# Normalization, the 1e-9 and three weight rebases moved to POOL in a windowed-attention stage

## The chip, the cores and the metric

The kernel runs on one NeuronCore of a Trainium2 chip. The metric is the device time of one execution in microseconds; less is better. A core has TensorE (PE in the profile), VectorE (DVE), ScalarE (ACT), GpSimd (POOL) and SyncE (SP), which here only issues transfers. Each engine runs its own instructions in order; between engines there are semaphores.

## The reference

Attention with a window of the last 96 positions and 8 global ones, then two feed-forward blocks:

```python
scores = scale * np.matmul(q, k.transpose(0, 1, 3, 2)) + bias      # masked to local | global
scores = scores - np.max(scores, axis=-1, keepdims=True)
a = np.exp(scores)
a = a / (np.sum(a, axis=-1, keepdims=True) + 1e-09)
x = np.matmul(a, v)                    # (2, 8, 768, 64) -> 1536 tokens x 512
h = x @ w_in                           # 512 -> 2048
g = np.where(h > 0.0, h, np.exp(np.minimum(h, 0.0)) - 1.0)
x = g @ w_out                          # 2048 -> 512
h = np.maximum(np.maximum(x @ w1, x @ w2), x @ w3)
out = h @ w_out2                       # 512 -> 768 -> 512
```

The weights arrive as 64-bit floats. The chip gets them as pairs of 32-bit words, rebuilds a 32-bit float from each pair and splits it into a high and a low part, whose products with the split activations make up the full-precision product.

## The kernel before, in words

**Attention steps.** The work is 48 steps; a step is one block of 128 queries of one head pair. The first 18 (k = 0 to 17) run in a loop of their own in `windowed` (from line 897), the first attention stage; the rest is woven into the feed-forward blocks by `run`, where TensorE has the long products. The schedule is manual: each engine gets its instructions in the order in which the code is written.

In the first stage a step is spread over four passes of the loop. In pass k TensorE makes the scores of step k in PSUM (`scores_pe`, L217), the product with the values of step k-3 (`values_pe`, L316) and the transposes of step k-2 (`turn_pe`, L287 or L293). DVE adds the biases and takes the row minimum (`scores_dve`, L243, one custom instruction and a short accumulator read for each of the two heads), forms the reciprocal of the sums of step k-1 (`recip`, L255), multiplies the exponentials of step k-1 by it (`norm`, L277, two instructions) and subtracts the rounded part of the output of step k-3 (`values_low`, L332). ACT rounds that output (`values_high`, L326), copies the transposes out of PSUM (`turn_act`, L304), exponentiates (`scores_act`, L264, with the row sums as accumulators) and adds 1e-9 to the two sums (`sums`, L226). POOL scales the queries of a later head pair every other step (`scale_queries`, L187).

**Weight conversion.** From pass 7 on, the generator `convert` hands out one piece per pass, for weight chunks 0, 1 and 2 (each 128 x 2 x 512 pairs of words). `c_rebase` (L404) multiplies the high words by a power of two, on ACT; `c_low` (L408) prepares the low words, on DVE; two `c_word` (L415, DVE, one long instruction each) join them and need the rebased high words; `c_high` (L423, ACT) rounds the high part; `c_rest` (L428, DVE) subtracts. The pieces fall so: pass 7 rebase and low of chunk 0; 8 and 9 the words; 10 high of 0 with rebase and low of 1; 11 word; 12 rest of 0; 13 word; 14 high of 1 with rebase and low of 2; 15 rest of 1; 16 and 17 words of 2. "High words" and "low words" are two interleaved halves of one buffer, so a rebase reads and writes every other 32-bit word.

**Later.** The products (L505) begin in pass 16. In the first feed-forward block POOL subtracts `gl` (L517), and conversion goes on there with rebases on ACT.

SP issues the loads in written order; query and key loads (`raw`), value loads (`v`) and weight chunks (`wr`) share its queue.

Of the kernel before, what the change touches and what calls it, by code (L numbers as in the profile page):

```python
# [16 lines left out]
AF = mybir.ActivationFunctionType  # L17
ALU = mybir.AluOpType
# [29 lines left out]
def numbers(nc, pool, n_ap):  # L48

    ni = pool.tile([P, 4], I32, name="ni")  # L50
    nc.sync.dma_start(ni, n_ap.bitcast(I32).partition_broadcast(P))
    w = pool.tile([P, 4], F32, name="nw")
    nc.vector.tensor_copy(w, ni)
    w2 = w.rearrange("p (a b) -> p a b", b=2)
    hi = pool.tile([P, 2], F32, name="nhi")
    nc.vector.scalar_tensor_tensor(
        hi, w2[:, :, 0], 0.0, w2[:, :, 1], op0=ALU.is_lt, op1=ALU.add
    )
    nf = pool.tile([P, 2], F32, name="nf")
    nc.vector.scalar_tensor_tensor(  # L60
        nf, hi, 4294967296.0, w2[:, :, 0], op0=ALU.mult, op1=ALU.add
    )
    return nf[:, 0:1], nf[:, 1:2]


def covered(nc, pool, ng, nl, flag):

    f = pool.tile([P, 4], F32, name="nok")
    nc.vector.tensor_scalar(f[:, 0:1], ng, 0.0, None, op0=ALU.is_ge)
    nc.vector.tensor_scalar(f[:, 1:2], ng, float(G), None, op0=ALU.is_le)  # L70
    nc.vector.tensor_scalar(f[:, 2:3], nl, 1.0, None, op0=ALU.is_ge)
    nc.vector.tensor_scalar(f[:, 3:4], nl, float(PREV + 1), None, op0=ALU.is_le)
    ok = pool.tile([P, 1], F32, name="ok")
    nc.vector.tensor_reduce(ok, f, axis=AX.X, op=ALU.min)
    nc.vector.tensor_copy(flag, ok)
# [33 lines left out]
class Windowed:  # L109
# [110 lines left out]
                )  # L220
            self.s_t[s] = [x[:, o:o + n] for x in sp]

    def sums(self, k):
        if k in self.p_t:
            m = self.p_t[k][1]
            self.nc.scalar.activation(m[:, 4:6], m[:, 2:4], AF.Copy, bias=1e-9)  # L226

    def scores_dve(self, k, early=False, other=-1):

# [36 lines left out]
                accum_out=m[:, 2 + u:3 + u],  # L266
            )

    def norm(self, k):
        if k not in self.p_t:  # L270
            return
        nc = self.nc
        n = self.geom(k)[-1]
        p, m = self.p_t[k]
        for u in range(2):
            o = slice(u * WIN, u * WIN + n)
            nc.vector.tensor_scalar(p[:, o], p[:, o], m[:, 6 + u:7 + u], None, op0=ALU.mult)  # L277

    def turn_pe(self, k, tag="TX"):
        if k not in self.p_t:  # L280
# [77 lines left out]
class Feed:  # L358
# [39 lines left out]
            return [(self.whole[c], slice(0, 2))]  # L398
        return [(self.wraw[j], j % 2) for j in (2 * c, 2 * c + 1) if j in self.wraw and c < NFC]

    def c_rebase(self, c):
        for r, _ in self.parts(c):
            a = r[..., 1].bitcast(F32)
            self.nc.scalar.activation(a, a, AF.Copy, scale=2.0 ** -112)  # L404

    def c_low(self, c):
        for r, _ in self.parts(c):
# [441 lines left out]
def windowed(tc, ctx, io, flag):  # L849
    nc = tc.nc  # L850
    f = Feed(tc, ctx, io)
    at = Windowed(tc, ctx, io, f.ps, f.xy, f.wt, f.act)
    with tc.manual_schedule():
        scratch = [f.cv.tile([P, 512], F32, tag="wr", name="sc") for _ in range(2)]
        at.load_pair(0, True)
        f.warm(WARM)
        at.positions(scratch)
        ng, nl = numbers(nc, at.const, io["nn"])
        for p in range(1, 3):
            at.load_pair(p, True)  # L860
        at.scale_queries(0)
        at.bases(ng, nl, 0, P + WIN)
        first = BLOCKS[0] // GRP * 8
        x = f.split_tiles()

        def convert():
            f.c_rebase(0)
            f.c_low(0)
            yield
            f.c_word(0, 0)  # L870
            yield
            f.c_word(0, 1)
            yield
            f.c_high(0)
            f.c_rebase(1)
            f.c_low(1)
            yield
            f.c_word(1, 0)
            yield
            f.c_rest(0)  # L880
            yield
            f.c_word(1, 1)
            yield
            f.c_high(1)
            f.c_rebase(2)
            f.c_low(2)
            yield
            f.c_rest(1)
            yield
            f.c_word(2, 0)  # L890
            yield
            f.c_word(2, 1)
            yield

        words = convert()
        h = f.ps.tile([P, 512], F32, tag="h", name="h")
        for k in range(first + 2):
            e = k % 2
            at.load_values(k, True)
            if e == 0:  # L900
                at.load_pair(k // 2 + 3, k < first)
                at.scale_queries(k // 2 + 1)
            if k <= first:
                at.scores_pe(k, (("S0", "S1"), ("y0", "y1"))[e], 1 + (k == first))
            if k >= first:
                f.product(h, f.w[0][:, 0], x, GRP, 0, (k - first) * 6, 6)
            at.values_pe(k - 3)
            at.turn_pe(k - 2, ("TX", "y2", "y3")[k % 3])
            if k < FILL[0]:
                f.fill(at.ident, FILL[1])  # L910
            at.scores_dve(k, True)
            at.values_high(k - 3, x)
            at.turn_act(k - 2, nc.scalar.copy)
            at.scores_act(k)
            at.sums(k)
            at.recip(k - 1)
            at.norm(k - 1)
            at.values_low(k - 3, x)
            if k >= CONV:
                next(words, None)  # L920
            if k in WLOAD:
                f.w_load()
        at.values_pe(first - 1)
        at.turn_pe(first, "TX")
        at.values_high(first - 1, x)
        at.turn_act(first, nc.scalar.copy)
        at.values_low(first - 1, x)
        at.recip(first + 1)
        at.norm(first + 1)
        next(words, None)  # L930
        f.run(at, first + 2, x, h, lambda: covered(nc, at.const, ng, nl, flag))


def build(tc, io):
    nc = tc.nc
    with tc.tile_pool(name="flag", bufs=1) as fp:
        flag = fp.tile([P, 1], I32, name="fast")
        with ExitStack() as ctx:
            windowed(tc, ctx, io, flag)
        fast = nc.values_load(flag[0:1, 0:1], min_val=0, max_val=1)  # L940
        with tc.If(fast < 1):  # L941
            with tc.tile_pool(name="xd", bufs=1, space=bass.MemoryType.DRAM) as dp:
                xd = dp.tile([NT // GRP, P, NCC, GRP], F32, name="xd")
                with ExitStack() as ctx:
                    dense_attention(tc, ctx, io, xd)
                with ExitStack() as ctx:
                    f = Feed(tc, ctx, io)
                    with tc.manual_schedule():
                        f.w_load()
                        f.w_load()  # L950
                        f.w_load()
                        for c in range(2):
                            f.c_rebase(c)
                            f.c_low(c)
                            f.c_word(c, 0)
                            f.c_word(c, 1)
                            f.c_high(c)
                            f.c_rest(c)
                        f.c_rebase(2)
                        f.c_low(2)  # L960
                        f.c_word(2, 0)
                        f.c_word(2, 1)
                        f.run(Stored(nc, f.xy, xd), 0)
# [73 lines left out]
```

## Time and profile before

| | |
|---|---|
| three runs | 569.23, 574.21, 575.95 us (median 574.21) |
| profiled execution | span 569.0 us; its own time is not listed beside the span |
| PE busy | 549.6 us (97%) |
| DVE busy | 315.4 us (55%) |
| ACT busy | 277.1 us (49%) |
| POOL busy | 78.3 us (14%) |
| first attention stage | about the first 50 us of the span |

The span runs from the first to the last instruction on the core. Busy shares are averages over the whole of it; the stage that is changed is less than a tenth. In rows of a timeline the first number is the start in microseconds from the span's start, the second the duration, and what stands in brackets at the end is the idle time of the engine before it and who ended it.

### The profile page before, as it was taken

To read this page: it belongs to the slowest core of one execution; us is meant where nothing else is said; L and a number is where in the kernel's file an instruction comes from. 1 tells how busy PE (TensorE), PEld (TensorE's weight loads), DVE (VectorE), ACT (ScalarE), POOL (GpSimd) and SP (SyncE) were. 2 spreads that over 40 slices of the span, in tenths; PEclk is the share of its full clock that TensorE was granted. 3 is DMA by queue.
4 is the path that set the end of the run, shared out by engine and by line. 5 is a ranking of instruction groups with operands and counts; after the bars stand their busy time and mean duration, and the time that the engine had idled before them with its cause. 6 is when DMAs were issued, how large, how long until landed. Compare 5 with 4: busy or idle time off the path is not lost. (4 is left out here: it accounts for less than half of the span.)

```text
span 569.0 us, 7586 instructions
## 1 busy us (share of the span) xinstructions
PE 549.6 (97%) x2772; PEld 435.0 (76%) x2772; DVE 315.4 (55%) x684; ACT 277.1 (49%) x622; POOL 78.3 (14%) x87
## 2 busy tenths in 40 slices
PE   8799999999999999999999999999999999999995
PEld 6467777776777777778888888888887888888884
DVE  6987999999745333333466656567754112312112
ACT  5988777777656555554555554524323101311011
POOL 4100222222210000000011222023320000000000
PEclk9969999999999999999999999999999999999999
DMA  8919444532211111010013223122302000010002
GB/s 293 381 45 345 166 168 137 181 122 78 67 36 42 42 41 43 20 55 1 0 38 111 88 98 111 37 75 77 117 29 75 1 1 0 8 67 1 0 1 79
DMA packets 16669, 46.61 MB, mean 82 GB/s; under 512 B 1776, under 2 KB 1776, under 8 KB 16624
## 3 DMA queue, kind: packets, MB, share of 16 engines
q1 hardware_dynamic: 15760, 44.47, 22.8%
q10 hardware_dynamic: 864, 1.57, 0.8%
q8 instruction: 24, 0.39, 0.3%
q14 instruction: 21, 0.17, 0.1%
HBM read 42.90 MB, written 3.15 MB: 81 GB/s over the span
## 5 line engine op out<-in xcount | busy, mean ns | idle before, releaser
L505 PE MATMUL h<-xh,w 128*128 128x512 f32 (+1 forms) x536 | 144.5, 391 | 0.8 <-ACT xh L485 0.8
L505 PEld LDWEIGHTS h<-xh,w 128*128 128x128 f32 x536 | 98.1, 188 | 24.5 <-issue 1.8
L536 PE MATMUL y<-gh,w 128*128 128x512 f32 x384 | 98.6, 399 | 0.0
L512 ACT CAST gh<-e 128x512 fp32r<-128x512 f32 x66 | 41.0, 622 | 101.8 <-DVE e L725 87.4
L536 PEld LDWEIGHTS y<-gh,w 128*128 128x128 f32 x384 | 69.7, 188 | 18.1 <-ACT e L526 1.7
L725 DVE TENSOR_TENSOR e<-S,e 128x512 f32<-128x512 f32 x36 | 24.9, 692 | 103.5 <-PE S L505 100.8
L505 PE MATMUL h<-xl,w 128*128 128x512 f32 (+1 forms) x268 | 81.8, 386 | 0.0
L505 PE MATMUL S<-xh,w 128*128 128x512 f32 x288 | 77.0, 389 | 0.0
L530 DVE SCALAR_TENSOR_TENSOR e<-e,h 128x512 f32<-128x512 f32 x48 | 33.0, 687 | 67.7 <-ACT e L526 67.7
L505 PEld LDWEIGHTS S<-xh,w 128*128 128x128 f32 x288 | 54.1, 188 | 11.2
L525 ACT ACTIVATE e<-h 128x512 f32<-128x512 f32 x48 | 28.7, 597 | 65.2 <-PE h L505 63.0
L462 POOL TENSOR_TENSOR w<-wr,w 128x512 fp32r<-128x512 f32 x24 | 35.4, 1474 | 166.1 <-ACT w L461 166.1
L505 PEld LDWEIGHTS h<-xl,w 128*128 128x128 f32 x268 | 50.0, 188 | 10.3
L517 DVE TENSOR_TENSOR gl<-e,gh 128x512 fp32r<-128x512 f32 x50 | 39.8, 796 | 31.8 <-ACT gh L512 31.6
L264 ACT ACTIVATE p<-p,m 128x232 f32<-128x232 f32 (+1 forms) x96 | 44.8, 469 | 24.4 <-DVE m L243 24.4
L544 PE MATMUL y<-gl,w 128*128 128x512 f32 x192 | 51.5, 390 | 0.0
L415 DVE SCALAR_TENSOR_TENSOR wr<-wr 128x1024 uint32<-128x1024 uint32 (+1 forms) x36 | 49.9, 1395 | 0.8 <-ACT wr L404 0.2
L505 PE MATMUL S<-xl,w 128*128 128x512 f32 x144 | 44.3, 389 | 0.0
L451 DVE SCALAR_TENSOR_TENSOR wr<-wr 128x512 uint32<-128x512 uint32 x48 | 43.0, 896 | 2.2
L544 PEld LDWEIGHTS y<-gl,w 128*128 128x128 f32 x192 | 36.0, 188 | 7.9 <-issue 0.3
L569 PE MATMUL y<-w,gh 128*128 128x512 f32 x144 | 37.3, 390 | 0.4 <-POOLq L941 0.4
L517 POOL TENSOR_TENSOR gl<-e,gh 128x512 fp32r<-128x512 f32 x16 | 21.0, 1310 | 104.3 <-ACT gh L512 104.3
(85 smaller groups left out, 604.4 us busy)
## 6 DMA issues: line engine op xcount, KB each, us to landing
wr<-wa SPq DMA_DIRECT2D x14, 1024.0 KB, 6.4
wr<-wb SPq DMA_DIRECT2D x24, 512.0 KB, 3.3
v<-v SPq DMA_DIRECT2D x24, 256.0 KB, 2.8
raw<-qk SPq DMA_DIRECT2D x16, 312.0 KB, 3.1
raw<-qk SPq DMA_DIRECT2D x8, 260.0 KB, 3.3
wr<-wa SPq DMA_DIRECT2D x4, 512.0 KB, 3.8
out<-ot ACTq DMA_DIRECT2D x6, 256.0 KB, 2.6
out<-ot SPq DMA_DIRECT2D x6, 256.0 KB, 2.5
```

The costliest lines, as they stand in the source:

```text
L264: self.nc.scalar.activation(p[:, o], p[:, o], AF.Exp, bias=m[:, u:u + 1], scale=-1.0, accum_out=m[:, 2 + u:3 + u],)
L415: self.nc.vector.scalar_tensor_tensor(r[..., 0], r[..., 1], v, r[..., 0], op0=op, op1=ALU.bitwise_or)
L451: self.nc.vector.scalar_tensor_tensor(t, a, c, t, op0=op, op1=ALU.bitwise_or)
L462: nc.gpsimd.tensor_tensor(w[:, j % 2, 1], v, w[:, j % 2, 0].bitcast(F32), op=ALU.subtract)
L505: nc.tensor.matmul(out[:, o:n], w[:, part % 2, c * P:c * P + P], (xl if part == 2 else xh)[:, c, o:n], start=c == 0 and part == 0, stop=c ...
L512: self.nc.scalar.copy(gh[:, 0:n], e[:, 0:n])
L517: (engine or self.nc.vector).tensor_tensor(gl[:, 0:n], e[:, 0:n], gh[:, 0:n].bitcast(F32), op=ALU.subtract)
L525: self.nc.scalar.activation(e, h, AF.Relu, scale=-1.0)
L530: self.nc.vector.scalar_tensor_tensor(e, e, -1.0, h, op0=ALU.add, op1=ALU.max)
L536: self.nc.tensor.matmul(y[e][:, 0:n], w[:, a, e * P:e * P + P], g[0][:, 0:n], start=fc == 0 and a == 0, stop=False,)
L544: self.nc.tensor.matmul(y[e][:, 0:n], w[:, 0, e * P:e * P + P], g[1][:, 0:n], start=False, stop=fc == NFC - 1,)
L569: nc.tensor.matmul(o[r], gh[:, r * P:r * P + P], w[:, a], start=j == 0 and a == 0, stop=False,)
```

## The change

In the loop of the first stage `sums`, `norm` and `c_rebase` get a flag that puts their instructions on POOL, as a tensor-scalar instruction with two operations; the operations are the same (add 1e-9, multiply by the reciprocal, multiply by 2 to the -112). `norm` of step k-1 now stands ahead of `sums` of step k in the written order. Steps from 18 on, and the normalization of step 17, which stands after the loop, are as before.

```diff
-    def sums(self, k):
+    def sums(self, k, early=False):
         if k in self.p_t:
             m = self.p_t[k][1]
-            self.nc.scalar.activation(m[:, 4:6], m[:, 2:4], AF.Copy, bias=1e-9)
+            if early:
+                self.nc.gpsimd.tensor_scalar(
+                    m[:, 4:6], m[:, 2:4], 1e-9, 1.0, op0=ALU.add, op1=ALU.mult
+                )
+            else:
+                self.nc.scalar.activation(m[:, 4:6], m[:, 2:4], AF.Copy, bias=1e-9)
...
-    def norm(self, k):
+    def norm(self, k, early=False):
...
-            nc.vector.tensor_scalar(p[:, o], p[:, o], m[:, 6 + u:7 + u], None, op0=ALU.mult)
+            if early:
+                nc.gpsimd.tensor_scalar(
+                    p[:, o], p[:, o], m[:, 6 + u:7 + u], 1.0, op0=ALU.mult, op1=ALU.mult
+                )
...
-    def c_rebase(self, c):
+    def c_rebase(self, c, early=False):
         for r, _ in self.parts(c):
             a = r[..., 1].bitcast(F32)
-            self.nc.scalar.activation(a, a, AF.Copy, scale=2.0 ** -112)
+            if early:
+                self.nc.gpsimd.tensor_scalar(
+                    a, a, 2.0 ** -112, 1.0, op0=ALU.mult, op1=ALU.mult
+                )
+            else:
+                self.nc.scalar.activation(a, a, AF.Copy, scale=2.0 ** -112)
...
-            f.c_rebase(0)
+            f.c_rebase(0, True)
...
-            f.c_rebase(1)
+            f.c_rebase(1, True)
...
-            f.c_rebase(2)
+            f.c_rebase(2, True)
...
             at.scores_act(k)
-            at.sums(k)
             at.recip(k - 1)
-            at.norm(k - 1)
+            at.norm(k - 1, True)
+            at.sums(k, True)
             at.values_low(k - 3, x)
```

POOL before: in the whole first stage its program holds the setup and then nothing but the query scalings, which run as far ahead as their loads allow.

```order
L103 MEMSET qsc 64x1 x8
masks.py:197 MEMSET ident 128x128
masks.py:199 AFFINE_SELECT ident<-ident 128x128
L187 TENSOR_SCALAR raw<-raw,qsc 128x256 x10
L517 TENSOR_TENSOR gl<-e,gh 128x512 x2
```

POOL now, from pass 6 to pass 10 (L283 is `norm`, L227 `sums`, L417 `c_rebase` in the changed file):

```order
L187 TENSOR_SCALAR raw<-raw,qsc 128x256
L283 TENSOR_SCALAR p<-p,m 128x232 x2
L227 TENSOR_SCALAR m<-m 128x2
L283 TENSOR_SCALAR p<-p,m 128x128 x2
L227 TENSOR_SCALAR m<-m 128x2
L417 TENSOR_SCALAR wr<-wr 128x1024
L187 TENSOR_SCALAR raw<-raw,qsc 128x256
L283 TENSOR_SCALAR p<-p,m 128x232 x2
L227 TENSOR_SCALAR m<-m 128x2
```

The scalings are now one per two steps among two normalizations and an addition per step, and a rebase stands between the addition of step 7 and the scaling and normalization of pass 8.

DVE before, in the second half of pass 7 and at the start of pass 8:

```order
L243 ISA p,m<-y_318,rel 128x232 [waits PE_49]
L243 ISA m 128x1
L255 RECIPROCAL m<-m 128x2 [waits Activation_49]
L277 TENSOR_SCALAR p<-p,m 128x128 [waits DVE_49]
L277 TENSOR_SCALAR p<-p,m 128x128
L332 TENSOR_TENSOR xl<-TX,xh 128x128 [waits Activation_49]
L408 TENSOR_SCALAR wr<-wr 128x1024 [waits DMAHW0_49]
L243 ISA p,m<-S_348,rel 128x232 [waits PE_49]
```

DVE now, from the conversion of pass 7 through pass 8 (L425 is `c_low`, L248 the scores, L260 `recip`, L344 `values_low`, L432 `c_word`):

```order
L425 TENSOR_SCALAR wr<-wr 128x1024 [waits DMAHW0_49]
L248 ISA p,m<-S_348,rel 128x232 [waits PE_49]
L248 ISA m 128x1
L248 ISA p,m<-S_349,rel 128x232 [waits PE_49]
L260 RECIPROCAL m<-m 128x2 [waits Pool_49]
L344 TENSOR_TENSOR xl<-y_323,xh 128x128 [waits Activation_49]
L432 SCALAR_TENSOR_TENSOR wr<-wr 128x1024 [waits DVE_49,Pool_49]
L248 ISA p,m<-y_373,rel 128x232 [waits PE_49]
```

The two normalizations are gone from DVE, its reciprocal waits for POOL where it waited for ACT, and the word conversion of pass 8 waits for POOL.

## Rows read from the trace of the kernel before

**Rows 1.** Stretches: us, busy of PE, PEld, DVE, ACT, POOL; PEclk, DMA share, GB/s.

```profile
10.00:20.00 10.00, 9.37 (x80) 5.44 (x78) 8.88 (x48) 9.76 (x41) 1.23 (x3) 1.00 1.04 405
20.00:30.00 10.00, 6.06 (x53) 3.73 (x54) 9.42 (x32) 9.38 (x30) 2.02 (x3) 1.00 0.82 315
30.00:40.00 10.00, 10.00 (x54) 6.08 (x53) 9.04 (x35) 7.58 (x26) 0.00 (x0) 0.52 0.16 60
```

**Rows 2.** Timeline of DVE, step 12, to the start of step 13.

```profile
30.10 0.39 DVE L243 CUSTOM_DVE_ANT_0 p<-S,rel 128x232 f32<-128x232 f32 x1
...
30.73 0.16 DVE L255 RECIPROCAL m<-m 128x2 f32<-128x2 f32 x1
30.93 0.59 DVE L277 TENSOR_SCALAR p<-p,m 128x232 f32<-128x232 f32 x2
31.44 0.28 DVE L332 TENSOR_TENSOR xl<-y,xh 128x128 fp32r<-128x128 f32 x1
31.64 1.22 DVE L428 TENSOR_TENSOR w<-wr,w 128x1024 fp32r<-128x1024 f32 x1
32.77 0.39 DVE L243 CUSTOM_DVE_ANT_0 p<-y,rel 128x232 f32<-128x232 f32 x1
```

**Rows 3.** Timeline of DVE: starts of steps 5, 7, 10 and 11, and ends.

```profile
13.80 0.39 DVE L243 CUSTOM_DVE_ANT_0 p<-y,rel 128x232 f32<-128x232 f32 x1
...
17.11 0.39 DVE L243 CUSTOM_DVE_ANT_0 p<-y,rel 128x232 f32<-128x232 f32 x1
...
24.75 0.39 DVE L243 CUSTOM_DVE_ANT_0 p<-S,rel 128x232 f32<-128x232 f32 x1
...
26.29 0.69 DVE L408 TENSOR_SCALAR wr<-wr 128x1024 uint32<-128x1024 uint32 x1
26.89 0.39 DVE L243 CUSTOM_DVE_ANT_0 p<-y,rel 128x232 f32<-128x232 f32 x1
...
47.59 0.28 DVE L332 TENSOR_TENSOR xl<-y,xh 128x128 fp32r<-128x128 f32 x1
```

**Rows 4.** Timeline of ACT and of DVE: an addition and a wait.

```profile
23.72 0.20 ACT L226 ACTIVATE m<-m 128x2 f32<-128x2 f32 x1
...
40.90 0.29 DVE L332 TENSOR_TENSOR xl<-y,xh 128x128 fp32r<-128x128 f32 x1 [1.40 <-ACT xh L326]
```

**Rows 5.** POOL: one line's durations (min/median/max ns), and an iota.

```profile
L187 POOL TENSOR_SCALAR raw<-raw,qsc x10: 477/522/934, 4.0 to 26.4; 128x256 f32<-128x256 f32 x10
...
1.67 0.14 POOL L79 IOTA rel<- 128x8 f32 x1
```

**Rows 6.** Timeline of DVE and POOL: conversions alone and beside POOL.

```profile
23.62 1.22 DVE L415 SCALAR_TENSOR_TENSOR wr<-wr 128x1024 uint32<-128x1024 uint32 x1
...
58.36 1.95 DVE L415 SCALAR_TENSOR_TENSOR wr<-wr 128x1024 uint32<-128x1024 uint32 x1
...
26.39 0.93 POOL L187 TENSOR_SCALAR raw<-raw,qsc 128x256 f32<-128x256 f32 x1 [1.02 <-DMA raw<-qk]
...
57.94 1.29 POOL L517 TENSOR_TENSOR gl<-e,gh 128x512 fp32r<-128x512 f32 x1 [5.27 <-ACT gh L512]
59.20 1.45 POOL L187 TENSOR_SCALAR raw<-raw,qsc 128x256 f32<-128x256 f32 x1
```

**Rows 7.** Timeline of PE: value products of five passes.

```profile
20.96 0.44 PE L316 MATMUL y<-p,v 128*64 128x128 f32 x4 [1.00 <-ACT p L304]
...
22.80 0.66 PE L316 MATMUL TX<-p,v 116*64 116x128 f32 x8 [0.22 <-ACT p L304]
...
24.71 0.66 PE L316 MATMUL y<-p,v 116*64 116x128 f32 x8
...
29.26 0.66 PE L316 MATMUL y<-p,v 116*64 116x128 f32 x8 [1.97 <-ACT p L304]
...
31.55 1.12 PE L316 MATMUL TX<-p,v 116*64 116x128 f32 x8
...
34.71 1.12 PE L316 MATMUL y<-p,v 116*64 116x128 f32 x8
```

More of the change, by code (lines that the diff above doesn't have):

```diff
@@ L276, in norm @@
             o = slice(u * WIN, u * WIN + n)
-            nc.vector.tensor_scalar(p[:, o], p[:, o], m[:, 6 + u:7 + u], None, op0=ALU.mult)
+            if early:
[3 more added lines that the diff above has]
+            else:
+                nc.vector.tensor_scalar(
+                    p[:, o], p[:, o], m[:, 6 + u:7 + u], None, op0=ALU.mult
+                )
     def turn_pe(self, k, tag="TX"):
@@ L399, in parts @@
         return [(self.wraw[j], j % 2) for j in (2 * c, 2 * c + 1) if j in self.wraw and c < NFC]
-    def c_rebase(self, c):
+    def c_rebase(self, c, early=False):
         for r, _ in self.parts(c):
             a = r[..., 1].bitcast(F32)
-            self.nc.scalar.activation(a, a, AF.Copy, scale=2.0 ** -112)
+            if early:
+                self.nc.gpsimd.tensor_scalar(
+                    a, a, 2.0 ** -112, 1.0, op0=ALU.mult, op1=ALU.mult
+                )
+            else:
+                self.nc.scalar.activation(a, a, AF.Copy, scale=2.0 ** -112)
     def c_low(self, c):
```

## The prediction, made before the changed kernel was run

> **What bounds the kernel now.** I read the table of 10 us windows first. After the first stage, which ends near 50 us, TensorE paces the kernel; the change touches only the 18 steps before. There [rows 1] ACT is busy 9.76 of 10 us between 10 and 20, DVE and ACT 9.4 each between 20 and 30, and between 30 and 40 TensorE is full, but at a granted clock of 0.52 (its lower level, 1.2 GHz); POOL is nearly free, and the DMA share falls from 1.04 to 0.16. So the bound changes hands: ACT up to step 7, then DVE, then TensorE at its low clock.
>
> Steps are read off DVE's first score instruction. Early ones go in pairs of 3.31 us, 13.80 to 17.11. From step 7 (17.11) each holds one weight-conversion instruction. A step with a long one (a word or a rest) [rows 2]: scores 0.63 us, reciprocal 0.20, two normalizations 0.51, `values_low` 0.20, conversion 1.13, together 2.67. One with the short `c_low` takes 2.14, from 24.75 to 26.89 [rows 3]. From step 7 to the last conversion's end at 47.59 are 30.48 us; three short and eight long steps would be 27.78. The 2.70 over are stalls, among them 1.40 in which DVE waited for ACT [rows 4], which had a weight cast and a rebase in front.
>
> **The sum is made on the profiled span.** That is 569.0 us; the profiled execution's own time is not listed apart from it. The span lies 0.2 under the fastest of the three times and 5.2 under their median, 574.21, to which I carry the difference. Within 1% (5.7 us) is about what a measurement of this kernel cannot tell from no change; the three times themselves spread by 6.7.
>
> **Part 1: what leaves DVE and ACT.** Seventeen steps lose 0.51 us of normalizing on DVE (the eighteenth stays there), eighteen a 0.20 us addition on ACT, and three a rebase on ACT [rows 2, 4]. In steps 3 to 6, ACT-bound, 0.2 a step comes off: **-0.8 us**. The bounds are 0 and -1.0: the longer way recip, normalize, transpose, next scores, can eat it.
>
> **Part 2: what POOL pays, and the port.** A 128x256 scaling in the same form (one tensor, a per-partition scalar, two operations) takes 0.477 us at its shortest [rows 5], so a 128x232 normalization about 0.44, two of them 0.8. The addition on two columns I put at the 0.14 of an iota on eight [rows 5]. The price depends on what POOL and DVE do to each other. Look at the three instructions at 58 us [rows 6]: DVE's word conversion, 1.22 us when alone, took 1.95 from 58.36, and ended 1.08 after POOL's 1.29 us subtraction ended at 59.23. POOL's next scaling was issued at 59.20 and ended 0.34 after the conversion did. At 26.39 a POOL scaling took 0.93 and ended 0.34 after DVE's `c_low` of 26.29 [rows 3, 6]. So the two shut each other out, instruction by instruction: the later one waits, loses about 0.14 less than the whole wait, and a waiting DVE instruction comes before POOL's next. DVE's scores, which read PSUM, ran beside POOL's subtraction unhurt.
>
> Now a long step by that rule, time 0 at the end of reciprocal(k-1). POOL normalizes head 0 from 0.1 to 0.55. DVE does `values_low` and reaches its conversion at 0.2, held until 0.55, and done 1.08 later at 1.63. Head 1 ends 0.34 after that, at 1.97, the addition at 2.1. DVE's next scores end at 2.18, reciprocal(k) at about 2.35. The step shrinks from 2.67 to 2.35, not to the 2.16 that removing 0.51 promises. With `c_low` it is 1.9 against 2.14. Eight times 0.32 and three times 0.24: **-3.3 us**. If POOL instead finished both heads before DVE got in, a long step would be 2.7 and this term near 0; if nothing collided, 8 x 0.51 + 3 x 0.51 = -5.6.
>
> The rows price a pair of normalizations at 0.8 us on POOL against 0.51 on DVE [rows 2, 5]. The Trainium skill, "GPSIMD Engine Reference", section 4.1, leaves elementwise work to VectorE, but calls POOL with one input roughly line-rate; at one element a cycle of its 1.2 GHz (section 1) a head would be an estimated 0.2 us, a long step about 2.1, and the sum 2 us lower. The trace's 0.477 us for 256 columns speaks against line rate. That POOL and VectorE share their SBUF interfaces (section 8) the 1.95 us shows.
>
> **Part 3: stalls that go.** The 2.70 us of stalls from step 7 on came from ACT's casts plus rebases and from the low clock. With the rebases gone from ACT they go: **-2.7 us** (the clock is a term of its own below). If only the 1.40 goes, -1.4.
>
> **Part 4: rebases on POOL.** A rebase is 1024 elements with a stride of 8 bytes. Four times 0.477 is 1.9 us; four times the 0.34 a released scaling needed, plus a start of 0.14, is 1.5; I take 1.65. The order says what waits. In step 7 the rebase follows the addition of step 7, which needs its exponentials, about 2.0 after reciprocal(6); so it runs from 2.0 to 3.65. Behind it on POOL stand the query scaling (0.48, every other step), normalization 7, addition 8. On DVE the word conversion of step 8 waits for the rebase itself, and reciprocal(8) for addition 8. After 3.65: scaling to 4.1, conversion to about 5.1, head 0, head 1, addition to 5.9, reciprocal done at 6.1. Step 8 therefore takes about 4.05 us instead of 2.35. Step 11 has no scaling: 3.75. Step 15's rest does not need the rebase's result, but meets it at the port: 3.75. Extra: 1.7 + 1.4 + 1.4, and 0.3 because the addition ends late in steps 7 and 10: **+4.8 us** (bounds +2.5, if POOL's rebase takes 1.0 us less than I think, to +8, if DVE waits out 2.6 us, twice the 1.29 of the 512-column subtraction).
>
> "GPSIMD Engine Reference", section 7, of the Trainium skill gives POOL reads of at most 8 bytes a step about 1.9 cycles per element and larger ones about 2.9; at 1.2 GHz an estimate of 1.6 or 2.5 us for this rebase, whose step is exactly 8 bytes. No run here shows a strided one; by 2.5 the sum would be 2.5 us higher.
>
> **Part 5: the clock.** A TensorE step takes 1.91 us at full clock (22.80 to 24.71) and 3.16 at half (31.55 to 34.71); it fell between 29.26, where an idle gap of 1.97 us ended, and 31.55 [rows 7], and was low to about 40 (0.52 in that stretch, [rows 1]). In step 8 of the changed kernel TensorE has done its values and sits about 2 us until normalization 7. The nearest row is that gap, so I assume one fall as before: step 9 costs 3.16 for 2.35, step 10 3.16 for 1.9, step 11 is slower anyway. **+2.1 us** (0 to +7).
>
> **Nothing else.** POOL's query scalings move behind the additions; the last was done at 26.39 [rows 6], and in the new order stands in step 16, so its data is long there. SP's loads keep their order and DMA has room from 30 us on [rows 1]. Everything later shifts with the stage. ACT's freed time hides behind DVE.
>
> Sum: -0.8 - 3.3 - 2.7 + 4.8 + 2.1 = +0.1. **Forecast 574.3 us, no change** (chance 0.45, 570 to 578).
>
> **Rivals.** (a) *The clock holds*: everything as above, no fall: 574.3 - 2.1 = 572.2. For it: a gap of 1.00 us that ended at 20.96 left the clock up [rows 7], and the 2 us of the new gap are worked out, not seen. Against it: the gap of 1.97 us was no longer. Chance 0.22. (b) *The port costs little, faster*: conversions run beside POOL. Long steps are 2.16, the rebases half hidden: -0.8 - 5.6 - 2.7 + 2.5 = -6.6, so 567.6. Against it: the 1.95 us [rows 6]. Chance 0.13. (c) *TensorE's clock stays low, slower*: each of the three rebase waits opens a gap, and the next comes before the clock is back. It decides if steps 9 to 17 all run at 3.16: steps 9, 12, 13, 16 and 17 lose 0.81 each, 10 and 14 1.26, and the products that follow lose 1.25 for each 1.91 us of work, say two such before the clock is back: 6.6 + 2.5 in place of the 2.1 above, 574.3 + 7.0 = 581.3. For it: one such gap kept the clock down for some 10 us before, and the waits here come 8 to 10 us apart. Against it: at the low clock TensorE is full, so the later waits open little. Chance 0.20, with POOL finishing two heads first (574.3 + 3.3 = 577.6) counted here. That the change does not do what it says is out: the order shows 34 normalizations, 18 additions and 3 rebases on POOL and none on the old engines in this stage.
>
> **How the numbers follow.** Under 568.5 lies most of (b) and a tail of (a): 0.14. Over 580 lies most of (c) and a tail of the forecast: 0.17. The rest is 0.69. The range 567.5 to 580.5 leaves out half of (b)'s and of (c)'s tails, under 0.2.
>
> **What would show it.** In the profile after: word and rest conversions of 1.4 to 1.6 us in steps 8 to 17, where they took 1.22; POOL rebases of 1.5 to 1.9; DVE's waits named POOL, three of 1 to 2 us each at steps 8, 11 and 15; a stretch at clock 0.5 beginning near 22 us. The prediction is wrong if conversions stay at 1.22 (then b), if the rebases take over 2.5, or if the clock is low beyond 35 us (then c).

## The result, and the profile after

The changed kernel takes 574.90 us (median of 20 runs, 573.41 to 578.21), the kernel before 570.87 (20 runs, 569.23 to 576.50). The ratio is 1.0072 with an interval of 1.0047 to 1.0096: some 4 us slower, within the 1% forecast as no change. The forecast of 574.3 lies 0.6 under the median, but by luck: it added +0.1 to a base of 574.21, and the measured difference is +4.0 on a base of 570.87. The times of most kernels here fall into two groups 3 to 5 us apart, the upper one with TensorE at half rate in the first steps wherever it was profiled, and of the three runs shown at first two lay in or near the upper one.

The profiles carry the mechanism. Profiled executions are compared below by the start of the last TensorE product, since what follows it is no part of the change: 562.29 before, 564.72 after, **+2.43 us**. The spans say +2.3 (569.0 and 571.3). Of the medians' +4.0 the profiles thus show 2.4; the profiled execution after is the fastest of its 20, the one before about a median one (below), and the other 1.6 are not explained here.

The head of the page after, engines with busy time, share of the span and instructions:

```profile
span 571.3 us, 7607 instructions
...
PE 550.4 (96%) x2772; PEld 433.5 (76%) x2772; DVE 308.0 (54%) x650; ACT 270.8 (47%) x601; POOL 108.0 (19%) x142
```

DVE lost 7.4 us of work, ACT 6.3, and POOL gained 29.7. Both relieved engines have room now, and the kernel is slower. The windows after, in the columns of [rows 1]:

```profile
10.00:20.00 10.00, 8.74 (x68) 4.48 (x66) 5.47 (x31) 7.67 (x32) 6.71 (x19) 1.00 1.03 403
20.00:30.00 10.00, 7.25 (x50) 4.02 (x50) 7.14 (x26) 6.11 (x24) 8.56 (x15) 0.82 0.83 309
30.00:40.00 10.00, 9.11 (x64) 5.16 (x64) 7.91 (x25) 7.03 (x24) 9.19 (x14) 0.84 0.17 62
...
26.00:33.00 7.00, 6.80 (x40) 4.11 (x40) 5.20 (x18) 5.34 (x17) 6.36 (x10) 0.53 0.37 138
```

In [rows 1] ACT, then DVE, is near full: 9.76, then 9.42. After, neither passes 7.91, and the only engines above 9 are POOL (9.19) and, in part at its lower clock, TensorE (9.11). POOL's share holds its waits at a port, as the rows below show. When no engine is full of work of its own and time is still lost, a circle of engines that wait for each other is to be looked for. The view of waits after, from 8 to 52 us, names one (us in total, times, longest):

```profile
DVE m L260 <- POOL m L227: 9.0, 18, 1.0
...
DVE xl L344 <- ACT xh L338: 1.8, 3, 0.7
```

DVE's reciprocal waits for POOL's addition 18 times. The timeline of DVE and POOL after shows both ends of that: two early steps, the step of the first rebase, a long step, two waits for ACT in steps 11 and 15, and the end of the stage.

```profile
13.54 0.17 DVE L260 RECIPROCAL m<-m 128x2 f32<-128x2 f32 x1 [0.98 <-POOL m L227]
...
17.21 0.19 POOL L227 TENSOR_SCALAR m<-m 128x2 f32<-128x2 f32 x1 [0.98 <-ACT xh L338]
17.43 0.17 DVE L260 RECIPROCAL m<-m 128x2 f32<-128x2 f32 x1 [1.04 <-POOL m L227]
...
17.95 0.89 POOL L283 TENSOR_SCALAR p<-p,m 128x232 f32<-128x232 f32 x2
...
21.38 1.13 POOL L417 TENSOR_SCALAR wr<-wr 128x1024 f32<-128x1024 f32 x1
22.55 1.49 DVE L432 SCALAR_TENSOR_TENSOR wr<-wr 128x1024 uint32<-128x1024 uint32 x1 [0.86 <-POOL wr L417]
...
25.11 0.17 DVE L260 RECIPROCAL m<-m 128x2 f32<-128x2 f32 x1 [0.43 <-POOL m L227]
25.37 1.98 POOL L283 TENSOR_SCALAR p<-p,m 128x232 f32<-128x232 f32 x2 [0.29 <-DVE m L260]
25.38 1.22 DVE L432 SCALAR_TENSOR_TENSOR wr<-wr 128x1024 uint32<-128x1024 uint32 x1
26.51 0.39 DVE L248 CUSTOM_DVE_ANT_0 p<-S,rel 128x232 f32<-128x232 f32 x1
...
27.43 0.19 POOL L227 TENSOR_SCALAR m<-m 128x2 f32<-128x2 f32 x1
27.66 0.17 DVE L260 RECIPROCAL m<-m 128x2 f32<-128x2 f32 x1 [0.43 <-POOL m L227]
...
30.92 0.29 DVE L344 TENSOR_TENSOR xl<-y,xh 128x128 fp32r<-128x128 f32 x1 [0.66 <-ACT xh L338]
...
41.77 0.29 DVE L344 TENSOR_TENSOR xl<-y,xh 128x128 fp32r<-128x128 f32 x1 [0.66 <-ACT xh L338]
...
47.24 1.98 POOL L283 TENSOR_SCALAR p<-p,m 128x232 f32<-128x232 f32 x2 [0.29 <-DVE m L260]
47.25 1.22 DVE L432 SCALAR_TENSOR_TENSOR wr<-wr 128x1024 uint32<-128x1024 uint32 x1
```

The long step is read from reciprocal to reciprocal, 25.11 to 27.66: 0.26 until POOL starts, 1.98 of two normalizations, 0.08 and an addition, and 0.23 after the addition's start the next reciprocal: 2.55 us. The pair alone takes 0.89 (17.95). Beside DVE's word conversion it takes 1.98, while the conversion keeps the 1.22 it had in [rows 6]: at the port it is POOL that waits, and POOL's wait lies on the circle. DVE's own work in that step would be 2.16 (the 2.67 of [rows 2] less 0.51 of normalizing).

That POOL is simply full does not explain this step: POOL stands idle for 0.29 before 25.37, waiting for DVE's reciprocal, and DVE for 0.43 before 27.66, waiting for POOL. In steps with a query scaling POOL has no idle time, and there the waits alone do not tell a circle from a full engine; the experiment with the addition back on ACT does.

The timeline of ACT and TensorE after, at the places that answer to [rows 7]:

```profile
14.56 0.86 PE L305 MATMUL y<-ident,p 128*116 128x128 f32 x4 [0.24 <-POOL p L283]
...
15.52 0.58 ACT L316 COPY p<-y 116x512 f32<-116x512 f32 x1 [0.83 <-PE y L305]
...
24.42 0.87 PE L305 MATMUL TX<-ident,p 128*116 128x128 f32 x4 [2.38 <-POOL p L283]
...
28.01 1.15 PE L217 MATMUL y<-raw 64*128 64x232 f32 x4
...
48.84 0.86 PE L305 MATMUL TX<-ident,p 128*116 128x128 f32 x4 [0.30 <-POOL p L283]
49.46 0.96 PE L522 MATMUL h<-xh,w 128*128 128x256 f32 x6
```

TensorE stands idle for 2.38 us before 24.42, where POOL does the rebase, a scaling and then the normalization of step 7. Its granted clock then falls to the lower level, 1.2 GHz (1.15 us at 28.01 for what takes 0.66 at the upper), for 26 to 33 us, where it was low for 30 to 40 before. And at the end the transposes of step 16 wait for POOL's pair of 47.24, with the products of the first feed-forward block behind them: 49.46, against 46.95 before.

Where the +2.5 us up to the first exponential of the feed-forward block (48.66 before, 51.17 after) arises, in starts of steps and the end of the last conversion (before 47.59 by [rows 3]; after 48.38, 1.13 behind its start at 47.25, as 26.51 stands 1.13 behind 25.38):

| stretch | before | after | difference |
|---|---|---|---|
| to step 3 | 10.49 | 10.41 | -0.08 |
| steps 3 to 6 | 6.62 | 7.40 | +0.78 |
| step 7 to the end of the last conversion | 30.48 | 30.57 | +0.09 |
| from there to the exponential | 1.07 | 2.79 | +1.72 |

### The profile page after: what moved, and what is told of

Its sections match the earlier page's. It is cut to its first block, busy times and chain, and to the rows that moved or that the text cites. A ratio compares the mean times of both kernels' runs of the same rounds, so it can differ in the third digit from the quotient of the medians.

```text
span 571.3 us, 7607 instructions
## 1 busy us (share of the span) xinstructions
PE 550.4 (96%) x2772; PEld 433.5 (76%) x2772; DVE 308.0 (54%) x650; ACT 270.8 (47%) x601; POOL 108.0 (19%) x142
## 5 line engine op out<-in xcount | busy, mean ns | idle before, releaser
L432 DVE SCALAR_TENSOR_TENSOR wr<-wr 128x1024 uint32<-128x1024 uint32 (+1 forms) x36 | 50.3, 1407 | 1.7 <-POOL wr L417 0.9
```

Source lines behind the costliest of these rows:

```text
L432: self.nc.vector.scalar_tensor_tensor(r[..., 0], r[..., 1], v, r[..., 0], op0=op, op1=ALU.bitwise_or)
```

## Experiments

Three theories stood against each other. **The circle**: reciprocal (DVE), normalization (POOL), addition (POOL), reciprocal closes on itself in every step, and is stretched where a conversion on DVE holds POOL's normalizations. **The rebases**: three long instructions at the head of POOL's queue hold everything, as Part 4 of the prediction has it. **The clock**: TensorE at its lower level is what costs. The lower level lasts 7 us in the changed kernel and 10 in the one before, which speaks against the clock as the main cause; what it costs in a step is read below. Each diff is against the changed kernel. Ratios are to the kernel before, timed beside each.

### One part put back

The rebases back on ACT:

```diff
-            f.c_rebase(0, True)
+            f.c_rebase(0)
```

(and so for chunks 1 and 2)

> The changed kernel with the three rebases back on ACT; normalization and addition stay on POOL. Theory A (a round trip through POOL sets the step: normalize k-2, transpose, ACT's copy, exponentials k, addition k, reciprocal k, normalize k; what lies on POOL or ACT in that circle counts in full): steps 8, 11 and 15, which took 3.95, 3.25 and 3.40 us, fall to about 2.7, but ACT's three rebases of 1.1 us push the exponentials behind them; 1 to 2 us less than the changed kernel, 2 to 3 us over the kernel before. Rival B (the rebases are the whole loss, the steps themselves gain): it gets to the time of the kernel before or 1 to 2 us under it.

574.03 us, ratio 1.0062 (1.0021 to 1.0102); last product at 564.71, where the changed kernel has 564.72; the 1 to 2 us expected did not come. So the rebases on POOL are not the loss: off POOL they cost as much on ACT. Its waits, from 8 to 52 us:

```profile
DVE m L260 <- POOL m L227: 7.8, 15, 1.0
...
POOL m L227 <- ACT xh L338: 6.5, 4, 2.2
```

POOL's addition now waits up to 2.2 us for ACT, which has the rebase ahead of the exponentials, and DVE's reciprocal behind it as before.

The addition back on ACT:

```diff
-            at.sums(k, True)
+            at.sums(k)
```

> The changed kernel with the addition of 1e-9 back on ACT; normalization and rebases stay on POOL. Theory A (round trip): the addition leaves POOL's part of the circle (0.19 us and a hand-over), but ACT gets its 0.20 back in the same circle; pairs of early steps go from 3.83 to 3.5 to 3.7 us, the stage is 1 to 3 us shorter than in the changed kernel. Rival C (it is the waiting for the port that counts, not the circle): the addition is a small instruction beside 0.9 us of normalization, under 0.5 us in all.

574.79 us, ratio 1.0044 (1.0003 to 1.0085). In its profiled execution TensorE has its lower clock from about 10 to 24 us (0.55, then 0.50), as in some executions of other kernels, so the median decides nothing; its 12 runs spread from 568.82 to 576.53, and the fastest is 4.6 under the fastest of the changed kernel. Its later steps, at the full clock, do tell something (DVE, two steps):

```profile
34.23 0.39 DVE L248 CUSTOM_DVE_ANT_0 p<-S,rel 128x232 f32<-128x232 f32 x1
...
34.87 0.15 DVE L260 RECIPROCAL m<-m 128x2 f32<-128x2 f32 x1
...
36.26 0.39 DVE L248 CUSTOM_DVE_ANT_0 p<-y,rel 128x232 f32<-128x232 f32 x1
...
38.33 0.40 DVE L248 CUSTOM_DVE_ANT_0 p<-S,rel 128x232 f32<-128x232 f32 x1
```

Long steps of 2.03 and 2.07 us, and a reciprocal that waits for nobody. With normalization on POOL but the addition off it, the circle is open, and a long step is what DVE's own work makes it. The step falls by 0.5 where POOL's work falls by the addition's 0.19, and POOL's pairs here stand back to back; so it is the circle, not a full POOL, that held DVE. In the two steps with the later rebases (3.96 and 3.81 us) part of that is given back; from step 8 to step 17 it takes 22.75 us, the changed kernel 25.82.

The normalization back on DVE:

```diff
-            at.norm(k - 1, True)
+            at.norm(k - 1)
```

> The changed kernel with the normalization back on DVE; addition and rebases stay on POOL. Theory A: the circle loses 0.9 us of POOL (nearly 2 us where a conversion keeps POOL out) and gains 0.5 to 0.6 of DVE; early pairs go back to 3.3 us, long steps are DVE's own 2.7; 2 to 4 us less than the changed kernel, so within 1 to 2 us of the kernel before. Rival (DVE is the bound and the move was a relief): 0.5 us a step more in steps 8 to 17, 3 to 5 us slower than the changed kernel.

570.65 us, ratio 1.0012 (0.9972 to 1.0052); last product at 563.00, 1.72 before the changed kernel's. Most of the +2.43 goes with this one edit. Its steps 7 to 17 take 26.71 us, as in the next kernel (26.81); the 1.5 us that it has more at the end of the stage fall in a stretch at the lower clock between 44 and 50 us.

The rebases alone on POOL, the other two put back:

```diff
-            at.norm(k - 1, True)
-            at.sums(k, True)
+            at.norm(k - 1)
+            at.sums(k)
```

> The kernel before with only the three rebases on POOL. Theory A: POOL is free when the rebase comes, so it runs 1.1 us early enough and nobody waits for it; ACT loses 3.4 us of work in three steps, where DVE had waited 0.44 and 1.40 us for ACT, and TensorE's idle gap before 29.26 shrinks: 1 to 3 us faster than the kernel before. Rival (the port makes the rebase as dear as on ACT): DVE's c_low or word is held up to 1.1 us three times and the time is that of the kernel before or up to 2 us over it.

569.29 us (10 of 12 runs from 568.8 to 569.9), ratio 0.9973 (0.9936 to 1.0010); last product at 560.84, 1.45 under the kernel before and 3.88 under the changed one. It is the best version here; that it beats the kernel before, the interval does not show. From step 8 to step 17 it takes 23.67 us where before took 25.64: DVE is busy throughout, and the stalls of ACT's queue are gone. POOL, with little else to do, runs the rebases ahead of need, at 12.21, 18.23 and 26.01. It pays in steps 7 and 10, 3.14 and 2.83 us for 2.17 and 2.14. The timeline of DVE and POOL there:

```profile
17.97 1.47 DVE L287 TENSOR_SCALAR p<-p,m 128x128 f32<-128x128 f32 x2
...
18.23 1.13 POOL L417 TENSOR_SCALAR wr<-wr 128x1024 f32<-128x1024 f32 x1
...
26.45 1.27 DVE L287 TENSOR_SCALAR p<-p,m 128x232 f32<-128x232 f32 x2
```

Here DVE waits: its pair, 0.48 alone, takes 1.47 beside the rebase.

### The suspected cost doubled, and taken away

The addition done twice:

```diff
             at.sums(k, True)
+            at.sums(k, True)
```

> The changed kernel with the addition of 1e-9 written twice in each of the 18 steps on POOL (the second repeats the first and gives the same value). On POOL the next instruction starts 0.28 us after an addition. Theory A (POOL's part of the circle normalize, add, reciprocal sets the steps): each step grows by 0.2 to 0.28 us, long ones from 2.55 to about 2.8, early pairs from 3.83 to 4.3; 3 to 5 us slower than the changed kernel. Rival C (DVE's held conversions set the steps and POOL waits in their shadow): under 1 us.

579.44 us (6 runs), ratio 1.0121 (1.0066 to 1.0176), 0.5% above the changed kernel's. Its profiled execution has TensorE at the lower clock in the early steps, as the one with the addition on ACT, so the size is read from a long step at the full clock (DVE and POOL):

```profile
40.65 0.47 POOL L227 TENSOR_SCALAR m<-m 128x2 f32<-128x2 f32 x2
41.16 0.17 DVE L260 RECIPROCAL m<-m 128x2 f32<-128x2 f32 x1 [0.71 <-POOL m L227]
...
43.99 0.17 DVE L260 RECIPROCAL m<-m 128x2 f32<-128x2 f32 x1 [0.71 <-POOL m L227]
```

The two additions take 0.47, 0.28 more than one; the step from reciprocal to reciprocal is 2.83, 0.28 more than 2.55; DVE's wait is 0.71, 0.28 more than 0.43. An instruction on two columns is paid in full, so the circle through POOL sets the long steps.

The six word conversions replaced by a maximum over the same 1024 columns, of the same length on DVE (the words of these chunks are then not joined):

```diff
+            if fake:
...
+                self.nc.vector.tensor_reduce(
+                    s, r[..., 1].bitcast(F32), axis=AX.XY, op=ALU.max
+                )
+                continue
...
-            f.c_word(0, 0)
+            f.c_word(0, 0, True)
```

(and so for the other five)

> The changed kernel with the six word conversions of the first stage replaced by a DVE maximum over the same 1024 high words, which reads one SBUF input and writes one column; the words of chunks 0 to 2 are left out, so the output is not the reference's. If a reduction takes as long as a word (1.1 to 1.2 us) and leaves the port to POOL, theory A says that a pair of normalizations beside it takes 0.9 us for 1.9, reciprocal no longer waits, and these steps fall from 2.55 to about 2.2, DVE's own work; six steps, 1.5 to 2.5 us under the changed kernel. Rival (POOL is slowed by any DVE traffic, or the steps are held elsewhere): pairs of 1.9 us and steps of 2.55 stay.

571.71 us, ratio 1.0026 (0.9996 to 1.0056); last product at 562.15, 2.57 under the changed kernel's. The timeline of DVE and POOL:

```profile
24.44 0.89 POOL L283 TENSOR_SCALAR p<-p,m 128x232 f32<-128x232 f32 x2 [0.46 <-DVE m L260]
24.45 1.21 DVE L434 TENSOR_REDUCE rd<-wr 128x1 f32<-128x1024 f32 x1
25.58 0.39 DVE L248 CUSTOM_DVE_ANT_0 p<-S,rel 128x232 f32<-128x232 f32 x1
...
32.96 1.33 DVE L451 TENSOR_TENSOR w<-wr,w 128x1024 fp32r<-128x1024 f32 x1
33.20 1.85 POOL L283 TENSOR_SCALAR p<-p,m 128x232 f32<-128x232 f32 x2
```

The same DVE time, begun in the same 0.01 us, and POOL's pair takes 0.89 instead of 1.98; that step is 2.03 us long (23.55 to 25.58). Beside the rest, which is still there, the pair is held as ever, 1.85. So it is not DVE's time but what the conversion does at the port that stretches the circle, and six conversions of that kind are worth the 2.6 us (the reduction too waits for the first rebase, 0.85 us, so that wait is not in the sum).

The Trainium skill ("SBUF — State Buffer", section "Who interferes with whom") says that VectorE and GpSimd share a pair of ports as an exclusive lock held for a whole instruction, that a VectorE instruction with two inputs in SBUF contends with a GpSimd instruction that reads there, and that a reduction never does on trn2. The 1.98 beside the conversion and the 0.89 beside the reduction agree with all three.

### Early and late apart

Normalization and addition on POOL only from pass 7 on, or only before pass 7 (in both the rebases stay on POOL):

```diff
-            at.norm(k - 1, True)
-            at.sums(k, True)
+            at.norm(k - 1, k >= CONV)
+            at.sums(k, k >= CONV)
```

and with `k < CONV` the other.

> The changed kernel with normalization and addition on POOL only from pass 7 on; the first seven passes as in the kernel before. Theory A: early pairs return to 3.31 us, step 7 starts at about 17.1 instead of 17.8, the rest stays: 0.7 to 1 us under the changed kernel, still 2.5 to 3.5 over the kernel before. Rival (the loss is made in the early steps): the time of the kernel before.

> The kernel with only the rebases on POOL, and besides normalization and addition on POOL in passes 0 to 6 alone. Theory A in its outer form (two steps round: normalize k-2, transpose, copy, exponentials k, add, reciprocal, normalize k): early pairs of 3.8 us where the kernel with the rebases alone has 3.4, step 7 at 17.8 for 17.1; 0.5 to 1 us slower than that kernel. Rival (the early passes are harmless): no difference.

| | median us | ratio | last product | over the rebases alone |
|---|---|---|---|---|
| rebases alone | 569.29 | 0.9973 (0.9936 to 1.0010) | 560.84 | |
| and early ones | 571.51 | 1.0017 (0.9984 to 1.0051) | 562.29 | +1.45 |
| and late ones | 572.18 | 1.0010 (0.9974 to 1.0046) | 563.31 | +2.47 |
| and both (the change) | 574.90 | 1.0072 (1.0047 to 1.0096) | 564.72 | +3.88 |

The two add up: 1.45 and 2.47 make 3.92. The early part is a loss where no conversion runs yet: 0.72 of its 1.45 arise in steps 3 to 6 (7.42 us for 6.70), the rest in steps 7 to 10, since all three rebases now run in steps 7 and 8. Its DVE timeline shows a pair of early steps of 3.83 us (14.12 to 17.95), where the same pair takes 3.30 with rebases alone, and the reciprocal behind POOL:

```profile
14.12 0.40 DVE L248 CUSTOM_DVE_ANT_0 p<-y,rel 128x232 f32<-128x232 f32 x1
...
17.58 0.17 DVE L260 RECIPROCAL m<-m 128x2 f32<-128x2 f32 x1 [1.05 <-POOL m L227]
...
17.95 0.40 DVE L248 CUSTOM_DVE_ANT_0 p<-y,rel 128x232 f32<-128x232 f32 x1
```

Of the late part 1.92 us arise between the start of step 17 and the first exponential (5.35 us, and 3.43 with rebases alone): the last conversion holds POOL's last pair, and the transposes and first products wait for it. With the reduction in the conversion's place that stretch falls from the changed kernel's 5.34 to 4.20 us.

### The early circle

In the early steps of the changed kernel POOL's addition itself waits 0.98 for ACT (17.21 above), and ACT waits 0.83 for transposes (15.52) that wait for POOL's normalization (14.56). That is a second circle: normalization of step k-2, its transposes, ACT's copy of them, which is written ahead of the exponentials of step k, their addition, the reciprocal. So ACT's order was exchanged, in the changed kernel and in the one with early ones only:

```diff
-            at.turn_act(k - 2, nc.scalar.copy)
-            at.scores_act(k)
+            at.scores_act(k)
+            at.turn_act(k - 2, nc.scalar.copy)
```

> The changed kernel with ACT's exponentials of step k written ahead of its copy of the transposes of step k-2, so that they no longer wait for POOL's normalization of step k-2. Theory A in its outer form (normalize k-2, transpose, copy, exponentials k, add, reciprocal, normalize k, two steps round): early pairs fall from 3.83 to 3.3 us or less; the long steps, where POOL waits out a conversion inside the shorter circle reciprocal, normalize, add, reciprocal, stay at 2.55 to 2.67; 1 to 2 us under the changed kernel. Rival (the early steps are lengthened by POOL's own work or by TensorE): pairs stay at 3.8, no change.

> As the run with normalization and addition on POOL in passes 0 to 6 alone, and ACT's exponentials of step k written ahead of its copy of the transposes of step k-2 in every pass. Theory A in its outer form: that cuts the circle, early pairs fall to 3.3 us or less and step 7 starts at about 17.0; 0.5 to 1 us faster than without the exchange. Rival (POOL's instructions themselves are too slow for the early steps): pairs stay at 3.8.

574.89 us, ratio 1.0051 (1.0014 to 1.0088), and 576.77, ratio 1.0110 (1.0077 to 1.0143). Neither shows the gain. In both profiled executions TensorE runs at half rate through just the steps that the edit is about, so the pairs cannot be read; the second is slower than without the exchange (ratio 1.0017), and why stays open. The windows of the second kernel:

```profile
10.00:16.00 6.00, 5.99 (x34) 3.08 (x32) 2.44 (x15) 3.31 (x13) 3.86 (x11) 0.58 1.03 407
16.00:24.00 8.00, 7.99 (x42) 4.85 (x42) 4.64 (x19) 4.77 (x19) 5.93 (x12) 0.50 0.82 311
```

That the early loss comes with POOL's normalization and addition is shown (the +1.45); that it closes through ACT's copy is read from the waits, and the experiment that should have opened the circle does not confirm it.

The reciprocal of step k-1 moved between the scores of the two heads of step k, so that POOL starts 0.3 us earlier:

```diff
-            at.scores_dve(k, True)
+            at.scores_dve(k, True, k - 1)
...
-            at.recip(k - 1)
```

> The changed kernel with DVE's reciprocal of step k-1 between the scores of the two heads of step k instead of behind both, so that POOL's first normalization runs beside the second head's scores, which do not use the port, and comes ahead of the conversion. Theory A: the inner circle starts 0.32 us earlier against the conversion; one normalization is done before it, long steps go from 2.55 to 2.3 to 2.45; 1 to 2.5 us under the changed kernel. Rival: the reciprocal now waits longer for the addition (DVE stands at it with the second scores behind it), and nothing is gained or up to 2 us lost.

574.96 us, ratio 1.0071 (1.0035 to 1.0107): no gain. On a circle it does not help to start one link earlier in DVE's order when the link waits for POOL; DVE's reciprocal then waits 1.13 in front of the second head's scores. Its profiled execution too has TensorE at half rate early, so no more is read from it.

### A version that might have been better

Rebases on POOL, addition on ACT, and from pass 7 on the second head normalized on ACT and the first on DVE:

```diff
+            if act and u:
+                nc.scalar.activation(p[:, o], p[:, o], AF.Copy, scale=m[:, 6 + u:7 + u])
...
-            at.norm(k - 1, True)
-            at.sums(k, True)
+            at.norm(k - 1, act=k >= CONV)
+            at.sums(k)
```

> The kernel with only the rebases on POOL, and from pass 7 on the second head's normalization on ACT as a copy with a per-partition scale, the first head's on DVE. By the profile with the rebases alone, DVE is full from step 7 on (2.67 and 2.14 us a step without a wait) and ACT has about 0.6 us a step to spare: steps fall by 0.25 us to about 2.4 and 1.9, 1.5 to 2.5 us faster than that kernel, 2.5 to 4 under the kernel before. Rival (ACT becomes the bound, or the normalization now waits behind the casts): no gain, or 1 us slower.

571.17 us, ratio 1.0054 (1.0021 to 1.0087). The timeline of DVE:

```profile
31.77 0.39 DVE L248 CUSTOM_DVE_ANT_0 p<-y,rel 128x232 f32<-128x232 f32 x1
...
34.19 0.39 DVE L248 CUSTOM_DVE_ANT_0 p<-S,rel 128x232 f32<-128x232 f32 x1
...
38.43 0.29 DVE L346 TENSOR_TENSOR xl<-y,xh 128x128 fp32r<-128x128 f32 x1 [0.64 <-ACT xh L340]
```

A long step is 2.42 us, 0.25 under 2.67, but step 15 is 3.69 (36.08 to 39.77), since ACT's cast of 1.12 us now stands with the normalization ahead of what DVE needs. The last product starts at 560.76, 0.08 before that of the rebases alone: no gain in the stage worth having. Its span is 1.3 us longer all the same: the last output transfer is issued at 561.80 and the span ends 7.2 us later, where with rebases alone 5.8 us follow 561.88. No engine works in that stretch; why it is longer stays open.

## Why the prediction was right, and where it was not

**The base.** The forecast stood on 574.21, the median of three, and the profiled span of 569.0 lay 5.2 below it. Other executions with spans of 568.9 to 569.2 took 570.7 to 571.3 us, about 2.0 more than the span. So the profiled execution took about 571.0, close to the median of the 20 runs. "The sum is made on the profiled span" was right, carrying the difference to 574.21 was not: 3.3 us of the forecast are this step, and they hide the +4.0 that the sum missed. With the base put right the forecast is 571.

**Part 1 failed in sign.** -0.8 for steps 3 to 6 was +0.78 (steps), with bounds of 0 and -1.0. The prediction took ACT as the bound there and 0.2 a step off it. It named the longer way "recip, normalize, transpose, next scores" as what can eat the gain, and did not follow it round: the addition stands behind the normalization on POOL, the reciprocal behind the addition, and ACT's copy behind the transposes (this last link is read from the waits and not confirmed). By the experiment with early ones only it costs 1.45, 0.72 of it in steps 3 to 6.

**Part 2 had the mechanism and the wrong one waiting.** Port and exclusion are as said, and the reduction in place of the conversion shows it. But the conversions did not take 1.4 to 1.6 us, they kept 1.21 to 1.25 but for 1.49 in step 8 and 1.34 in step 16, and by the prediction's own test that meant rival (b), a cheap port. It meant that POOL waits: 1.98 for 0.89. The long step was forecast at 2.35 and is 2.55 to 2.67; with `c_low`, at 1.9 and is 2.15 (step 14). The term is not -3.3: the five long steps without a rebase lost 0.12, 0.05, 0.12, 0.00 and 0.12, together 0.41 where five times 0.32 was promised. The prediction had a long step of 2.7 and a term near 0 only for the case that POOL finished both heads before DVE got in; it came near that with DVE first.

**Part 3 held only with the rebases alone.** There the stalls of ACT's queue went: 1.97 us less than before from step 8 to 17, and 0.3 less behind it. In the changed kernel DVE's waits for ACT's rounding add up to 1.8 us, as before (0.44 and 1.40): 0.66 each in steps 11 and 15, where ACT has a weight cast of 1.11 in front (from 29.61 and 40.47), and 0.50 behind the last conversion. The same casts make no such wait with the rebases alone, so it is not the rebases that keep them; ACT's copies stand behind transposes that wait for POOL, which is the likely reason, though no run shows it by itself.

**Part 4 was right in step 8 and too dear.** Steps 8, 11 and 15 are the long ones, as forecast, with 3.95, 3.25 and 3.40 us for 4.05, 3.75 and 3.75. But DVE waits for a rebase only in step 8, 0.86 us at 22.55; in steps 11 and 15 it waits 0.66 for ACT's rounding (30.92, 41.77), and the conversion behind that is held 0.2 at most. A rebase takes 1.13, not 1.65. The 768 columns that it has more than a scaling cost (1.13 - 0.48)/768, 0.85 ns each; without a stride a pair of 128x232 normalizations takes 0.89 and a pair of 128x128 ones 0.72, 0.82 ns for each column more: the stride of 8 bytes costs next to nothing. By the Trainium skill, "GPSIMD Engine Reference", section 7, the prediction had an estimate of 1.6 for it; the trace does not agree.

**Part 5 was right in its place and too dear.** The gap forecast as about 2 us is 2.38, and the clock falls behind it, once. It is low for 7 us, and shows most in step 10, 2.68 us against 2.15 in the like step 14: about 0.5, not 2.1.

**"Nothing else" failed.** +1.72 us, most of the loss in the profiles, arise behind the last conversion, where the prediction had "everything later shifts with the stage". The last conversion holds POOL's last pair, and TensorE's transposes and the first products stand behind it.

From step 7 on to the last conversion the terms sum to +0.9 and +0.09 was measured, but by errors that cancel: rebases and clock too dear, long steps and ACT's stalls too cheap. That the sum comes out near is luck. The forecast of no change by 1% was right; the reading that nothing is lost was wrong.

## What to carry to other kernels

When work goes to a third engine, follow each result round until it comes back to the instruction that started it: relieved engines and none full of its own work are a hint of a circle, and on a circle even a 0.19 us instruction is paid in full. Of two engines at a shared port ask which one waits, and what is behind that one; move to POOL what nobody waits for within the step (the rebases), not a link between two DVE instructions. And put a forecast on the profiled execution's own time, or on the median of many runs, not on the median of three.

## What the runs showed of the hardware that was not expected

- Where a POOL instruction and a two-input DVE instruction start within 0.01 us of each other (25.37 and 25.38, 47.24 and 47.25), DVE kept its 1.22 us and POOL took 1.98, although POOL's start stands first in the trace. With POOL under way, DVE waited: 1.47 for 0.48 with the rebases alone, where its second multiplication started at 18.26, 0.03 behind the rebase of 18.23.
- POOL's rate is 0.85 ns a column above a start, in a strided rebase as in a scaling (256 columns 0.48, 1024 columns 1.13), and 0.19 on two columns. The Trainium skill, "GPSIMD Engine Reference", section 3.1, gives 1.03 cycles an element for simple bodies; at its 1.2 GHz that is an estimated 0.86 ns, and the trace agrees.
- TensorE ran at half rate in the early steps of some executions, and the clock's column did not always say so. In the kernel with the exponentials first (windows, then TensorE):

```profile
10.00:16.00 6.00, 5.99 (x32) 3.52 (x30) 2.19 (x15) 3.92 (x17) 3.57 (x10) 1.00 1.03 409
```

```profile
15.37 1.15 PE L217 MATMUL y<-raw 64*128 64x232 f32 x4
```

  The column reads 1.00 and the scores take 1.15 us for 0.66. So the clock is better read from a known matmul's duration beside the column. Five profiled executions have that half rate (addition on ACT, reciprocal early, addition twice, and the two with exponentials first); what starts it was not found.
